# One pool of eight PSUM banks, and exponentials over any two of them, in an attention + Mish kernel

## The chip, the cores and the metric

The kernel runs on one core of a Trainium2 chip. The engines are TensorE (PE), VectorE (DVE), ScalarE (ACT), GpSimd (POOL) and SyncE (SP, which only issues DMAs here). PE writes its results to PSUM, which has eight banks of 512 float32 columns on each of 128 partitions; ACT and DVE read PSUM, POOL works on SBUF only. Each engine has its own instruction stream, which it works off in order, and the streams are tied together by semaphores. The metric is the device time of one execution in microseconds: 779.48 us, the median of three runs (779.46 to 780.76). The profiled execution took 773.49 us, with a span of 771.7 us from its first to its last instruction.

## The reference

With x of 2048 x 640, 32 heads of 20 columns, and a Mish feed-forward of width 1536:

```python
qkv = (x @ wqkv)                        # 640 -> 3 * 640, 32 heads of 20
scores = einsum("bhqd,bhkd->bhqk", q, k) * 20 ** -0.5
a = (softmax(scores) @ v) @ wo
h = x @ w1 + b1                         # 640 -> 1536
b = (h * tanh(softplus(h))) @ w2        # Mish, 1536 -> 640
g = sigmoid((x * gate_w).sum(-1))
out = g * a + (1 - g) * b
```

Softmax takes an exponential of 32 x 2048 x 2048 scores. That is the bulk of the element work, and it is what the change touches.

## The kernel before

**Tiling of the attention.** Heads are taken four at a time (p, eight quads), queries in chunks of 512 (c, four of them); a pair (p, c) is a group, 32 in all. For each of 16 key tiles (kt) the four heads of a group give four score tiles of 128 keys x 512 queries, each one PSUM bank. The scores of the four heads run on PE as four 32-row tiles of the array. Two heads' tiles make a unit: a slot of two neighbouring banks, 128 x 1024 float32. There are 1024 units.

**Two ways to an exponential.** A unit goes either to ACT, which takes the exponential of both banks in one instruction of 1024 columns (`poll_act`, L835, into a slot of `EA`), or to DVE, which writes a bit pattern that is a piecewise-linear exponential (`psum_chord`, L853, into `EC`); POOL then adds a constant twice to make two shifted copies (`gp_chord`, L864), and the three pieces are summed by PE like three key tiles. The latter are called chords below. 736 units go to ACT and 288 to DVE.

**PV.** PE multiplies the exponentials by V (`emit_pv`), four heads side by side as four 32-column tiles, and adds into one bank; a column of ones in `VA` yields the softmax denominators. DVE copies the bank out at the end of a group (L876).

**Banks before.** The eight banks have fixed uses: slots 0, 1 and 2 are banks 0-1, 2-3 and 4-5; bank 6 (`ACCB`) sums PV; bank 7 (`MISC`) takes all other matmuls (projections, w1, w2, wo, transposes), called pieces. In the opening banks 4 and 5 are lent to the pieces. All eight are parts of one tile, `K.ps`, and `EA` (8 slots) and `EC` (9) are two tiles.

**What sets the order.** `make_plan` plays the whole kernel through on a clock of assumed durations: `poll_pe`, `poll_act`, `poll_dve`, `poll_gp` and `poll_sp` each pick what their engine starts next, and `emit` records it. The recorded order is the order of the instructions in every stream. Waits are not written by hand: the framework compares the regions that instructions read and write, in program order, and puts semaphores where it finds a conflict. For PSUM it works by bank, and keeps apart two engines' accesses to one bank, two reads as well.

**Opening.** x comes in by five SP DMAs; PE transposes it (L240) and DVE copies it to `xT` (L245). The weights come through ACT's DMA queue (L1129 to L1139). `K_pad0` (L199) on DVE spreads the first quad's weights to 32-column strips before PE can make the first keys and queries. POOL fills `VA` with ones and clears `kT` and `qT`.

Of the kernel before, what the change touches and what calls it, by code (L numbers as in the profile page):

```python
# [10 lines left out]
P = 128  # L11
# [16 lines left out]
MISC, ACCB = 7, 6  # L28
NEA, NCH = 8, 9
# [22 lines left out]
for _c in range(NQC):  # L52
    GROUPS += [(6, _c), (7, _c)]
NG = len(GROUPS)
NU = NG * 32
# [3 lines left out]
    "thr": 326.27,  # L59
    "lead": 216.34,  # L60
    "dvw": 64.38,
    "gpmax": 2746.83,
    "gptwo": 3121.26,
    "urgent": 24.71,
    "kq": 3.96,
# [3 lines left out]
    "h0": 3.84,  # L69
    "h1": 14.84,  # L70
    "w0": 9.5,
    "w1": 21.29,
    "hl": 6.15,
    "wl": 5.27,
# [4 lines left out]
XAT = [3300.0, 4300.0, 6300.0, 8400.0, 10500.0]  # L79
# [66 lines left out]
def uinfo(n):  # L146
    g, k = divmod(n, 32)
    p, c = GROUPS[g]
    return g, p, c, k // 2, k % 2


def make_plan(K, par):
# [4 lines left out]
    stat = dict(act=0, dve=0, gp2=0, s4=0, s2=0, pv4=0, pv2=0, fill=0)  # L157
# [33 lines left out]
    pl.at(5500.0, lambda: dve_q.append(("fn", 950.0, K_pad0, lambda: pl.give("w0"))))  # L191
    pl.at(9000.0, lambda: pl.give("wv0"))
    pl.at(14000.0, lambda: pl.give("wk", "wq"))
    pl.at(18000.0, lambda: pl.give("wv"))
    pl.free["SP"] = 4000.0

    def K_pad0():
        for raw, dst in ((K.wk0, K.wkp), (K.wq0, K.wqp)):
            K.nc.vector.tensor_copy(  # L199
                out=dst.rearrange("p k (r d) -> p k r d", r=4)[:, :, :, 0:DH],  # L200
                in_=raw.rearrange("p k (r d) -> p k r d", r=4),
            )
# [118 lines left out]
    def add_v(j, t0, due):  # L321
# [18 lines left out]
        for i in range(nt):  # L340
            for kt in range(KT):
                pieces.append((max(w / 2.4, 50.0) + 2.0, "C", (lambda b, i=i, kt=kt: pc(i, kt, b)), ()))
# [48 lines left out]
    def add_wo(t, half, due):  # L391
        c, c0 = t // 4, half * 320

        def pc(j, b):
            n = 96 if j == 3 else P
            l = K.onc[0:n, c % 2, j, (t % 4) * P : (t % 4 + 1) * P]
            mm4(bank(b)[:, 0:320], l, K.wop[0:n, j, c0 : c0 + 320], j == 0, j == 5)
# [84 lines left out]
    ring_free = [0, 1]  # L482
    lent = [4, 5]
    misc_free = [MISC] + lent
    opn = {"lent": True, "tail": False, "back": 0}
    filled, flying = [], []
    land = [0.0]
    pair_free = {}
    eafree = list(range(NEA))
    ecfree = list(range(NCH))  # L490
    nxt, pv_g = [0], [0]
    acc_free = [True]
    pv_pend = {g: ([], []) for g in range(NG)}
    pv_left = {g: [16, 16] for g in range(NG)}
    nchord = {g: [0, 0] for g in range(NG)}
    first_w = {}
    mode = [None]
    recent = []
    tailq = []

# [6 lines left out]
    def unit_ready(n):  # L507
        g, p, c, kt, pair = uinfo(n)
        return ("k", p, kt // 4) in pl.tok and ("q", p, c) in pl.tok

    def emit_score(n, slot):
        g, p, c, kt, pair = uinfo(n)

        def fn():
            for t in range(2):
                r = 2 * pair + t
                mm(
                    K.ps[:, 2 * slot + t, :],
                    K.kT[32 * r : 32 * r + 32, p % 3, kt * P : (kt + 1) * P],
                    K.qT[32 * r : 32 * r + 32, p % 3, c * QC : (c + 1) * QC],  # L520
                    True,
                    True,
                    (32 * r, 0),
                )

        emit(fn)

    def scored(ns):
        for n, s in ns:
            flying.remove(n)  # L530
            filled.append((n, s))
            if n % 32 == 31:
                pl.give(("sdone", n // 32))

    def hurry():

        if filled or flying:
            return False
        ta = pl.free["ACT"]
        t2 = min(list(pair_free.values()) or [0.0])  # L540
        sw = 0.0 if mode[0] == "R" else 105.0
        if max(t2, pl.t) + 440.0 + sw <= ta + par["thr"]:
            return False
        return pl.t + 440.0 + sw + par["lead"] >= ta

    def try_score(idle=False):
        n = nxt[0]
        if n >= NU or not ring_free or not unit_ready(n):
            if n < NU and ring_free and n not in blk:
                blk[n] = [pl.t, pl.t]  # L550
            return False
        if n in blk:
            blk[n][1] = pl.t
        if len(ring_free) < 2 and not idle and not hurry():
            return False
        k = 1
        if n + 1 < NU and len(ring_free) >= 2 and unit_ready(n + 1):
            k = 2
        ns = [(n + i, ring_free.pop(0)) for i in range(k)]
        for u, s in ns:  # L560
            emit_score(u, s)
            flying.append(u)
        land[0] = pl.t + 440.0 + (105.0 if mode[0] != "R" else 0.0) if k == 2 else 0.0
        nxt[0] = n + k
        stat["s4" if k == 2 else "s2"] += 1
        pe_run("R", 217.0, lambda: scored(ns))
        return True

    def pv_usable(e):
        g, p, c, kt, pair = uinfo(e[0])  # L570
        return ("v", 0 if p == 0 else (1 if p < 4 else 2), kt) in pl.tok

    def emit_pv(g, items):
        if g not in first_w:
            first_w[g] = set()
            acc_free[0] = False
        todo = []
        for t in range(2):
            for pair, e in items:
                n, ap, rel, last = e  # L580
                _, p, c, kt, _ = uinfo(n)
                r = 2 * pair + t
                fin = last and pv_left[g][pair] == 1 and not pv_pend[g][pair]
                todo.append((r, kt, 4 * p + r, ap, t, r not in first_w[g], fin))
                first_w[g].add(r)

        def fn():
            for r, kt, h, ap, t, first, fin in todo:
                mm(
                    K.ps[32 * r : 32 * r + 32, ACCB, :],  # L590
                    K.VA[:, kt, h * VS : h * VS + 32],
                    ap()[:, t * QC : (t + 1) * QC],
                    first,
                    fin,
                    (0, 32 * r),
                )
# [3 lines left out]
        def done():  # L600
            for pair, e in items:
                e[2]()
                if e[3]:
                    pv_left[g][pair] -= 1
            if pv_left[g] == [0, 0] and pv_g[0] == g:
                pv_g[0] = g + 1
                gtimes.append(pl.t)
                dve_q.append(("acc", g))

        stat["pv4" if len(items) == 2 else "pv2"] += 1  # L610
        pe_run("C", 217.0, done)

    def try_pv(single=False):
        g = pv_g[0]
        if g >= NG or (g not in first_w and not acc_free[0]):
            return False
        items = [(pair, pv_pend[g][pair][0]) for pair in range(2) if pv_pend[g][pair] and pv_usable(pv_pend[g][pair][0])]
        if not items:
            return False
        if len(items) < 2 and not single and pv_left[g][1 - items[0][0]] > 0:  # L620
            return False
        for pair, e in items:
            pv_pend[g][pair].pop(0)
        emit_pv(g, items)
        return True

    def try_misc(lim):
# [3 lines left out]
        if not misc_free or lim is None:  # L631
            return False
        for k, m in enumerate(misc[:40]):
            if m.due > nxt[0] + lim:
                break
            if pl.has(m.need):
                if hasattr(m, "key"):
                    if not stg_free:
                        continue
                    stg_of[m.key] = stg_free.pop(0)  # L640
                misc.pop(k)
                m.bank = misc_free.pop(0)
                started.append(m)
                return run_piece(m)
        return False

    def run_piece(m):
# [11 lines left out]
        pe_run(md, dur, done)  # L659
        return True  # L660

    def lent_back():
        opn["back"] += 1
        if opn["back"] == 2:
            ring_free.append(2)

    def misc_done(m):
        b = m.bank
        if b in lent and not opn["lent"] and not opn["tail"]:
            lent_back()  # L670
        else:
            misc_free.append(b)
        pl.give(*m.gives)
        if m.name == "xt15":
            opn["lent"] = False
            for x in [x for x in misc_free if x in lent]:
                misc_free.remove(x)
                lent_back()
        if m.name.startswith("w2."):
            for q in range(2):  # L680
                if ("w2done", q) not in pl.tok and all(("w2e", t, hh) in pl.tok for t in range(8 * q, 8 * q + 8) for hh in range(2)):
                    pl.give(("w2done", q))
                    if q == 1:
                        load_wo()
# [497 lines left out]
```

## Time and profile before

| | us |
|---|---|
| median of three runs | 779.48 |
| profiled execution / its span | 773.49 / 771.7 |
| ACT busy | 719.0 (93%) |
| PE busy (matmuls are pipelined, ends modelled) | 736.6 (95%) |
| POOL busy | 665.6 (86%) |
| DVE busy | 499.1 (65%) |
| ACT: 736 exponentials, mean 1041 ns each, together | 689.1 |
| DVE: 288 chords, mean 1223 ns each | 351.8 |
| POOL: 576 shifted copies, mean 1047 ns each | 602.9 |

The mean of one instruction is from its start to its end; successive exponentials overlap a little, so 736 of them take 689.1 us, or 0.936 us each. A busy share says how long an engine had something in flight. For PE it is larger than the time in which PE streams columns, since a matmul's end is modelled and four small tiles run side by side. What an engine waited for is read from the idle time before its instructions.

### The profile page before, as it was taken

Reading aid. Unit: us, or ns where it says so; the run is one execution under the profiler, and the core shown is the slowest. Engines: PE = TensorE matmul, PEld = TensorE weight load, DVE = VectorE, ACT = ScalarE, POOL = GpSimd, SP = SyncE. Lnnn points to the kernel's source line nnn. Section 1 sums busy time; section 2 is a strip of 40 time slices with the busy share of each in tenths; the row PEclk is TensorE's granted clock in tenths of the full one; section 3 lists DMA queues with packets and bytes.
Section 4 is the critical chain, followed back from the end, with each engine's and each line's share of the span. In section 5 each row is a group of like instructions: output and inputs, shape, how many; then the busy total and the mean of one; then the engine's idle time right before and its main releaser. Section 6 shows DMA issues by size and latency. Waiting matters only on the chain.

```text
span 771.7 us, 24991 instructions
## 1 busy us (share of the span) xinstructions
PE 736.6 (95%) x10492; PEld 261.3 (34%) x10492; DVE 499.1 (65%) x588; ACT 719.0 (93%) x757; POOL 665.6 (86%) x627
## 2 busy tenths in 40 slices
PE   4899999999999999999999999999999999999996
PEld 2333332332233433333233323224333333333234
DVE  5676566666667666676656667667666655666573
ACT  1599999999999999999999999999999999999992
POOL 9378777889888999899999878988999999999994
PEclk9999999999999999999999999999999999999999
DMA  9231211110111010111211111012201003122112
GB/s 294 95 119 59 79 41 31 41 38 21 34 27 41 23 29 20 44 40 34 80 29 29 33 50 38 17 27 74 82 28 48 25 28 89 50 76 68 58 52 79
DMA packets 45682, 41.86 MB, mean 54 GB/s; under 512 B 20080, under 2 KB 39200, under 8 KB 45568
## 3 DMA queue, kind: packets, MB, share of 16 engines
q1 hardware_dynamic: 40976, 37.59, 16.5%
q10 hardware_dynamic: 4592, 2.66, 1.2%
q8 instruction: 82, 1.34, 0.7%
q14 instruction: 32, 0.26, 0.1%
HBM read 27.59 MB, written 12.38 MB: 52 GB/s over the span
## 4 chain that ended last, share of the span: by engine, by line
PE 59%; POOL 20%; ACT 7%; DVE 5%; issue 5%; DMA 3%; SPq 0%; DVEq 0%; POOLq 0%; ACTq 0%
PE ps L230 59%; POOL EC L864 19%; ACT EA L835 7%; DVE EC L853 3%; DMA b1bf<-in_B_b_dram 2%; POOL ons L1014 1%; DVE accs L876 1%; DMA act<-in_A_x_dram 1%; POOL R L1014 0%; PE ps L240 0%; DVE act L353 0%; DVE stg L285 0%; DMA den<-accs 0%; SPq L993 0%; DVE ost L400 0%
## 5 line engine op out<-in xcount | busy, mean ns | idle before, releaser
L835 ACT ACTIVATE EA<-ps 128x1024 bf16<-128x1024 f32 x736 | 689.1, 1041 | 35.9 <-PE ps L230 31.9
L864 POOL TENSOR_SCALAR EC<-EC 128x1024 uint16<-128x1024 uint16 x576 | 602.9, 1047 | 92.8 <-DVE EC L853 46.7
L853 DVE TENSOR_SCALAR EC<-ps 128x1024 uint16<-128x1024 f32 x288 | 351.8, 1223 | 203.3 <-PE ps L230 129.2
L230 PE MATMUL ps<-qT,kT 32*128 32x512 bf16 x2048 | 289.1, 384 | 7.7 <-ACT EA L835 4.1
L230 PE MATMUL ps<-EC,VA 128*32 128x512 bf16 x1728 | 237.7, 384 | 6.2 <-POOL EC L864 4.6
L230 PE MATMUL ps<-EA,VA 128*32 128x512 bf16 x1472 | 210.2, 384 | 0.4 <-DVE accs L876 0.2
L230 PEld LDWEIGHTS <-kT 32*128 32x128 bf16 x2048 | 77.2, 91 | 253.6 <-issue 250.3
L230 PEld LDWEIGHTS <-VA 128*32 128x32 bf16 x3200 | 82.6, 94 | 113.8 <-issue 98.9
L230 PE MATMUL ps<-R,act 128*32 128x320 bf16 x1536 | 83.0, 302 | 0.3 <-DVE bst L372 0.3
L230 PE MATMUL ps<-xT,R 128*32 128x512 bf16 x960 | 77.1, 383 | 0.6 <-DVE act L353 0.3
L230 PEld LDWEIGHTS <-R 128*32 128x32 bf16 (+1 forms) x1728 | 41.2, 95 | 45.5 <-issue 33.1
L230 PEld LDWEIGHTS <-act 128*32 128x32 bf16 x1536 | 37.0, 95 | 32.0 <-issue 24.2
L353 DVE TENSOR_SCALAR act<-ps,b1f 128x512 bf16<-128x512 f32 x48 | 35.8, 746 | 8.5 <-PE ps L230 8.4
L230 PE MATMUL ps<-R,R 128*32 128x320 bf16 (+1 forms) x768 | 40.0, 302 | 0.5 <-DVE R L974 0.5
L230 PE MATMUL ps<-wv,xT 128*32 128x81 bf16 (+2 forms) x960 | 34.2, 257 | 0.9 <-DVE kT L262 0.5
L285 DVE CAST stg<-ps 128x512 bf16<-128x512 f32 (+1 forms) x40 | 27.3, 683 | 10.9 <-PE ps L230 10.5
L230 PE MATMUL ps<-xT,wk 128*32 128x512 bf16 (+1 forms) x360 | 32.5, 383 | 0.8 <-DVE bst L372 0.3
L1014 POOL TENSOR_TENSOR ons<-accs,rb 128x512 bf16<-128x512 f32 x24 | 30.6, 1275 | 2.0
L230 PE MATMUL ps<-xT,wq 128*32 128x512 bf16 x400 | 31.2, 383 | 0.4 <-DVE VA L332 0.4
L876 DVE COPY accs<-ps 128x512 f32<-128x512 f32 x32 | 21.9, 685 | 7.9 <-PE ps L230 7.5
L230 PEld LDWEIGHTS <-xT 128*32 128x32 bf16 x960 | 18.5, 96 | 13.6 <-issue 11.7
L372 DVE TENSOR_SCALAR bst<-ps,og 128x320 bf16<-128x320 f32 x32 | 17.4, 544 | 8.7 <-PE ps L230 8.0
(62 smaller groups left out, 179.1 us busy)
## 6 DMA issues: line engine op xcount, KB each, us to landing
rb<-rd_d SPq DMA_DIRECT2D x124, 64.0 KB
qd<-stg SPq DMA_DIRECT2D x20, 128.0 KB
b_d<-bst SPq DMA_DIRECT2D x16, 160.0 KB
bst<-b_d SPq DMA_DIRECT2D x16, 160.0 KB
out_dram<-ost SPq DMA_DIRECT2D x16, 160.0 KB
kT<-kd SPq DMA_DIRECT2D x28, 80.0 KB
qT<-qd SPq DMA_DIRECT2D x28, 80.0 KB
kd<-stg SPq DMA_DIRECT2D x16, 128.0 KB
```

The source lines that it names most:

```text
L230: K.nc.tensor.matmul(o, lhsT=l, rhs=r, start=first, stop=last, tile_position=pos, skip_group_check=True)
L285: K.nc.vector.tensor_copy(out=K.stg[0:w, s, :], in_=bank(b)[0:w, :])
L353: K.nc.vector.tensor_scalar(out=K.act[:, f, (c % 2) * QC : (c % 2 + 1) * QC], in0=bank(b), scalar1=K.b1f[:, f : f + 1], scalar2=None, op0= ...
L372: K.nc.vector.tensor_scalar(out=K.bst[:, t % 3, c0 : c0 + 320], in0=bank(b)[:, 0:320], scalar1=K.og[:, t : t + 1], scalar2=None, op0=ALU.mult,
L835: lambda: K.nc.scalar.activation(K.EA[:, e, :], K.ps[:, 2 * slot : 2 * slot + 2, :].rearrange("p b n -> p (b n)"), ACT.Exp, scale=SCALE)
L853: lambda: K.nc.vector.tensor_scalar(out=K.EC[:, e, :], in0=K.ps[:, 2 * slot : 2 * slot + 2, :].rearrange("p b n -> p (b n)"), scalar1=CH_M ...
L864: K.nc.gpsimd.tensor_scalar(out=K.EC[:, e, :], in0=K.EC[:, e0, :], scalar1=float(CH_ADD[k]), scalar2=1.0, op0=ALU.add, op1=ALU.mult)
L876: emit(lambda: K.nc.vector.tensor_copy(out=K.accs[:, g % 2, :], in_=K.ps[:, ACCB, :]))
L1014: gp_q.append((1350.0, lambda: K.nc.gpsimd.tensor_tensor(out=dst(), in0=K.accs[:, b, :], in1=K.rb[:, b, :], op=ALU.mult), lambda: pl.give( ...
```

## The change

It does five things.

1. Scores are handled by the bank. A unit is now one head's tile in one bank (2048 units). All eight banks are one list, `pool`: scores, pieces and the PV sum take banks from it as they come free, up to four scores a visit of PE.
2. An ACT exponential takes any two filled banks with one instruction, by a stride between them: `K.ps[:, b0 : b1 + 1 : b1 - b0, :]`. Its output goes to any two slots likewise.
3. A chord is one bank on DVE (128 x 512); two of them share one POOL instruction per shifted copy, over two slots with a stride.
4. `EA` and `EC` become one tile `E` of 35 slots of 512 columns.
5. Opening: the spreading of the first weights goes from DVE to ACT, ahead of ACT's later DMA issues; POOL sets only the `VA` columns that V does not overwrite; the clearing of rows 96 to 127 of `onc` and of the same rows of `wop` is new on POOL, and wo's pieces use all 128 rows.

The parameters of the plan change with it. Cut to its core:

```diff
-MISC, ACCB = 7, 6
-NEA, NCH = 8, 9
+NE = 35
-NU = NG * 32
+NU = NG * 64
...
-    pl.at(5500.0, lambda: dve_q.append(("fn", 950.0, K_pad0, lambda: pl.give("w0"))))
+    pl.at(5800.0, lambda: pl.give("w0"))
...
-    ring_free = [0, 1]
-    lent = [4, 5]
-    misc_free = [MISC] + lent
+    pool = list(range(8))
...
-    def emit_score(n, slot):
+    def emit_score(n, b):
...
+            mm(
+                bank(b),
...
     def try_score(idle=False):
...
+        k = len(pool)
+        g = pv_g[0]
+        if g not in accb:
+            k -= 1
+        if not started and next_misc(par["resv"]) is not None:
+            k -= 1
+        k = min(k, 4)
...
+        while len(ns) < k and n + len(ns) < NU and unit_ready(n + len(ns)):
+            ns.append((n + len(ns), pool.pop(0)))
...
     def poll_act():
-            emit(
-                lambda: K.nc.scalar.activation(
-                    K.EA[:, e, :], K.ps[:, 2 * slot : 2 * slot + 2, :].rearrange("p b n -> p (b n)"), ACT.Exp, scale=SCALE
-                )
-            )
...
+            us = sorted((filled.pop(0) for _ in range(min(2, len(filled)))), key=lambda x: x[1])
+            es = sorted(efree.pop(0) for _ in us)
+            k, b0, b1, e0, e1 = len(us), us[0][1], us[-1][1], es[0], es[-1]
+
+            def fn():
+                src = K.ps[:, b0 : b1 + 1 : max(b1 - b0, 1), :]
+                dst = K.E[:, e0 : e1 + 1 : max(e1 - e0, 1), :]
+                K.nc.scalar.activation(dst, src, ACT.Exp, scale=SCALE)
...
-                in0=K.ps[:, 2 * slot : 2 * slot + 2, :].rearrange("p b n -> p (b n)"),
+                K.nc.vector.tensor_scalar(
+                    out=K.E.bitcast(U16)[:, es[k][i], :],
+                    in0=K.ps[:, b, :],
...
     def gp_chord(src, dst, k):
         K.nc.gpsimd.tensor_scalar(
+            out=slots(dst), in0=slots(src), scalar1=float(CH_ADD[k]), scalar2=1.0, op0=ALU.add, op1=ALU.mult
...
-    tl("EA", [P, NEA, 2 * QC], BF16)
-    tl("EC", [P, NCH, 2 * QC], U16)
+    tl("E", [P, NE, QC], BF16)
...
     nc.scalar.activation(K.dmy, K.dmy, ACT.Exp)
+    for raw, dst in ((wk0, K.wkp), (wq0, K.wqp)):
+        nc.scalar.activation(
+            dst.rearrange("p k (r d) -> p k r d", r=4)[:, :, :, 0:DH],
+            raw.rearrange("p k (r d) -> p k r d", r=4),
+            ACT.Copy,
+        )
     nc.scalar.dma_start(K.wv[:, :, 0:V0], cols(2 * D, 2 * D + V0))
...
-    nc.gpsimd.memset(K.VA[:, 0:4, :], 1.0)
-    nc.gpsimd.memset(K.VA[:, 4:16, :], 1.0)
+    nc.gpsimd.memset(K.VA[:, :, 0 : H * VS].rearrange("p t (h d) -> p t h d", d=VS)[:, :, :, DH:VS], 1.0)
+    for h in (4, 16, H):
+        nc.gpsimd.memset(K.VA[:, :, h * VS : h * VS + 12], 1.0)
```

How the instructions count, before and after, in the built programs:

| engine, work | before | after |
|---|---|---|
| ACT exponentials | 736 of 1024 columns | 732 of two banks, 3 of one |
| of these over neighbouring banks | 736 | 144 |
| DVE chords | 288 of 1024 | 647 of 512 (66 banks get two) |
| POOL shifted copies | 576 of 1024 | 547 of two slots, 2 of one |
| PE scores, matmuls / visits | 2048 / 710 | 2048 / 729 |
| PE PV matmuls | 3200 | 3210 |
| PE matmuls by zero (fills) | 72 | 36 |

## The prediction

> **What bounds the kernel now.** I read the busy shares first, then the groups of instructions, then ACT's own timeline.
>
> ```profile
> PE 736.6 (95%) x10492; PEld 261.3 (34%) x10492; DVE 499.1 (65%) x588; ACT 719.0 (93%) x757; POOL 665.6 (86%) x627
> ...
> L835 ACT ACTIVATE EA<-ps 128x1024 bf16<-128x1024 f32 x736 | 689.1, 1041 | 35.9 <-PE ps L230 31.9
> ...
> L876 DVE COPY accs<-ps 128x512 f32<-128x512 f32 x32 | 21.9, 685 | 7.9 <-PE ps L230 7.5
> ```
>
> PE's 95% is modelled overlap: 20 matmuls of 512 columns at 29.07 below take 1.25 us, four abreast, so a row of four streams for (1.25 - 0.39) / 4 = 0.215 us. All matmuls of the kernel before at that rate (by width) stream for 536 us. ACT is the bound: 689.1 / 736 = 0.936 us per exponential, idle only 35.9 us ahead of them, of which these rows of its timeline show the large part:
>
> ```profile
> 17.50 1.94 ACT L835 ACTIVATE EA<-ps 128x1024 bf16<-128x1024 f32 x2 [14.20 <-PE ps L230]
> 22.10 5.60 ACT L835 ACTIVATE EA<-ps 128x1024 bf16<-128x1024 f32 x6 [2.67 <-PE ps L230]
> 34.15 17.12 ACT L835 ACTIVATE EA<-ps 128x1024 bf16<-128x1024 f32 x18 [6.44 <-PE ps L230]
> ...
> 407.29 88.34 ACT L835 ACTIVATE EA<-ps 128x1024 bf16<-128x1024 f32 x94 [0.29 <-PE ps L230]
> ```
>
> From 34 to 755 us ACT is 98% busy. It runs 94 exponentials without a stop because PE, DVE and ACT work on different slots at the same time. So what can be won is the opening and some 12 us of small gaps; what can be lost is that overlap.
>
> **The change part by part.**
>
> *Counts.* ACT: 732 exponentials of two banks and 3 of one for 736, 732 x 0.936 + 3 x 0.5 = 686.7, -2.4 us. The strided form has no row; the nearest are Mish over 12 runs of 256 columns (four in 10.72 us at 245.82, 0.87 ns per column and row) and the exponential itself (0.936 us per 1024, 0.91 ns). The runs cost Mish nothing to be seen; I take 0, ends -10 and +35 us (0.05 us on 669). DVE: 647 chords at the 0.685 us of the 512-column copy above are 443 us for 351.8, +91; DVE then works 586 of 771 us, hidden behind ACT's 98%; were ACT faster it would be next. POOL: 548 copies for 576 at 1.047 us, -29 us, hidden; its new small memsets (1.49 us for the 1536 columns at L1144) are covered by that. PE: 2.5 more PV rows, 9 fewer fills, 19 more score visits at 0.1 us: under 2 us. All hidden as long as ACT's stream runs on.
>
> *Opening.*
>
> ```profile
> 7.10 4.92 DVE L199 COPY wkp<-wk 128x400 bf16<-128x400 bf16 x1
> ...
> 12.07 2.33 PE L230 MATMUL ps<-xT,wkp 128*32 128x512 bf16 x20 [3.18 <-DVE wkp L199]
> ...
> 17.40 0.45 PE L240 MATMUL ps<-ident,act 128*128 128x128 bf16 x5
> 20.54 0.44 PE L240 MATMUL ps<-ident,act 128*128 128x128 bf16 x5 [2.69 <-DVE xT L245]
> ...
> 29.07 1.25 PE L230 MATMUL ps<-xT,wkp 128*32 128x512 bf16 x20
> ```
>
> The first keys wait for the DVE copy until 12.02. On ACT two copies of 400 columns cost about 0.5 us each (ACT's 320-column `otmp` takes 0.53) once the weights have landed, between 4 and 7.1 us; PE could begin at 7.2, when the first four tiles of `xT` are done: -4.9 us. Of the gaps of 2.67 and 6.44 us, which wait for later keys, between none and all may go: I take -3, so -8 in all, ends 0 and -14. ACT's five weight DMAs (L1135 to L1139) now stand behind the copies, 4 to 6 us later; the first use of `wq` and `wv` was at 28 and 31 us, so this hides. POOL's shorter memsets end earlier, but its first chord came only at 31 us: 0.
>
> *The waits that strided exponentials bring.* This is the large term. The framework makes a wait from regions. I read, in the order of the built program, which instruction each wait names. An exponential over banks b0 and b1 is guarded as if it touched every bank between them. 588 of the 735 exponentials have banks in between. One place shows it: exponential 362 reads banks 1 and 7 and waits for the last PV matmul put into bank 5 before it; the next PE instruction in order, a w2 matmul into bank 4, waits for exponential 362 to end, and so does DVE's next chord, of bank 6; exponential 363 (banks 0 and 3) waits for scores that stand behind that w2 matmul, and for a chord of bank 2 that stands behind the chord of bank 6. PE and DVE work in order, so everything behind the waiting instruction waits too.
>
> To count it, I followed from each exponential all waits back through the other engines (with what stands ahead in their order) to the newest exponential that must have ended. Before: that is the one just ahead for 3 of 736, two back for 606, three for 125. After: just ahead for 517 of 735, two back for 207. With the same order but each bank guarded for itself, it would be 3 and 674. So in 517 places ACT must end, another engine must do its piece, and only then ACT goes on. The prices:
>
> ```profile
> 35.07 3.77 ACT L835 ACTIVATE EA<-ps 128x1024 bf16<-128x1024 f32 x4
> ...
> 36.14 0.39 PE L230 MATMUL ps<-qT,kT 32*128 32x512 bf16 x2 [0.15 <-ACT EA L835]
> ```
> ```profile
> 545.91 0.39 PE L230 MATMUL ps<-qT,kT 32*128 32x512 bf16 x2
> ...
> 546.40 1.02 ACT L835 ACTIVATE EA<-ps 128x1024 bf16<-128x1024 f32 x1 [0.38 <-PE ps L230]
> ```
> ```profile
> 759.49 0.40 PE L230 MATMUL ps<-EC,VA 128*32 128x512 bf16 x4
> ...
> 759.94 0.69 DVE L876 COPY accs<-ps 128x512 f32<-128x512 f32 x1 [3.63 <-PE ps L230]
> ```
>
> The first exponential of the row at 35.07 lasts 1.02 us, to 36.09, and the score that waits for it starts at 36.14: from ACT's end to PE's start 0.05 us. From PE's start to the reader's start it is 0.45 us (0.49 and 0.45 here). An exponential lasts 1.03 us from start to end.
>
> - 371 places by PE alone. Their stretches of PE, from the first instruction that waits for the old exponential to the one that the new one waits for, hold 2,482 matmuls, 157.5 us of streaming, 0.425 each. Pitch: 1.03 + 0.05 + (0.425 - 0.215) + 0.45 + 0.07 for a change between score and other tiles (a score visit of 0.39 is followed after 0.32, not 0.215) = 1.81 instead of 0.936: 0.87 x 371 = 323 us.
> - 79 by PE and then DVE: 1.03 + 0.05 + 0.55 + 1.1 chords x 0.69 + 0.05 = 2.43, 1.49 x 79 = 118 us.
> - 40 by one DVE read: 1.85, 0.91 x 40 = 36 us.
> - 27 by two or three DVE reads: about 1.64 x 16 + 2.7 x 11 = 56 us.
>
> Together +533 us. Lower end: shortest exponential (1.006), no passing time, 0.43 from PE to ACT, no change of tiles: 1.64 and 2.13, 1.70, 2.4, loss 261 + 94 + 31 + 40 = +426. It can't be less while the waits are in the program. Upper end: the stretches may in turn wait for DVE, POOL or slots (POOL's copies now often wait for PE to free a slot: 411 waits on PE for 25), and the 207 places two back may lose something: I allow 0.25 us on all 735, +180.
>
> The Trainium skill, "PSUM — Partial Sum Buffer", on bank collisions, says to guard PSUM by bank and quadrant, and that accesses to different banks run clean. By that rule the banks in between need no guard; guarded so, the order would have 3 such places, and the sum would be the third rival's.
>
> Sum: 771.7 - 2.4 - 8 + 533 + 2 = 1296 us of span. The profiled time stands 1.8 us above its span and the median 6 us above that: 1304. Rounded 1300. Ends: 771.7 - 13 - 14 + 426 + 8 = 1179; two thirds of the upper allowance, 120 us, make 1420.
>
> **The rivals.**
>
> 1. *The same alternation, and PE falls to its slow rate as well.* Two rows of 20 equal matmuls above differ: 2.33 us after 3 us without a matmul, 1.25 later. PE streams 544 of 1300 us (42%). Against: after a gap of 2.69 us at 20.54 five transposes took 0.44, as before it, and the new gaps are about 1 us. Slow for half the time, the stretches (239 us of streaming in all classes, and 0.2 more on 470 ends) cost +165: 1465. The Trainium skill, "TensorE: Matmul & The Clock Gate", Part 1: The HAM clock gate, has the clock drop after an idle window of 3.4 us; by that gaps of 1 us keep it up, and the row at 20.54 agrees.
> 2. *Cheaper alternation.* Many of the waits named may be met by the time they are read, if PE and DVE lag less than the program allows. Against: in these 517 places the chain starts at the end of the exponential just ahead, so nothing can be early. Half price would be 1040.
> 3. *Faster.* The guards in between don't act at run time, and the opening decides: 779.5 - 8 - 2.4 - some 6 of the small gaps = 763. It decides when fewer than some 15 exponentials pay 0.87 us. For it: nothing in the rows; the waits of the kernel before are in its trace (596 waiting instructions on ACT, of 603 in its program).
> 4. *DVE the bound, no guards.* 586 us on DVE plus its waits for PE (129.2 before): about 790.
>
> **How the numbers follow.** Forecast 0.80, rival 1 0.07, rival 2 0.07, rival 3 0.05, rival 4 0.01. The range 1180 to 1420 is the forecast's own. Faster by over 0.2%: 0.05; within 0.2%, about what a measurement here can tell from no change: 0.01; slower: 0.94.
>
> **What would show it.** ACT idle some 500 us ahead of the exponentials, released by PE and DVE; PE idle ahead of matmuls "<-ACT", in the before 4.3 us, now hundreds; rows of one to three exponentials instead of 94; one exponential still 1.03 us; PE's rows of 20 at 1.25 us; the first exponential before 14 us. The prediction is wrong if ACT's rows are as long as before, or if the strided exponential itself lasts longer.

## The result, and the profile after

The changed kernel takes 1615.1 us, the median of four runs (1613.8 to 1621.9), beside 779.5 us for the kernel before on the same chip: 2.074 times as long, with a 95% interval of 2.067 to 2.080. The forecast was 1300 with a range to 1420. The direction was right, and the size was missed by 315 us. One of the ten executions of the first experiment's kernel below took 1038.5 us at a mean clock of 0.56, and its ratio leaves that one out.

The profiled execution has a span of 1612.0 us. Its page, first the busy shares and the granted clock of TensorE in 40 slices (5 is half speed), then the costliest groups with their idle time ahead:

```profile
PE 1180.3 (73%) x10466; PEld 305.0 (19%) x10466; DVE 579.5 (36%) x945; ACT 777.4 (48%) x758; POOL 629.6 (39%) x604
...
PEclk8755567576666755555565775575657555556767
...
L849 ACT ACTIVATE E<-ps 128x1024 bf16<-128x1024 f32 x735 | 746.2, 1022 | 815.1 <-PE ps L233 616.4
...
L988 DVE TENSOR_SCALAR E<-ps 128x512 uint16<-128x512 f32 x647 | 434.4, 688 | 829.9 <-PE ps L233 619.5
```

The idle time ahead of ACT's exponentials has grown from 35.9 to 815.1 us, which is 779 of the 840 us that the span has grown by. One exponential still lasts 1.02 us, as one by itself did before (the row at 546.40 in the prediction), so the strided form itself costs nothing. No engine is busy throughout: PE's 73% holds matmuls that last longer (a PV matmul 0.55 us on average for 0.38), since the mean clock of the execution is 0.623 (0.999 before). The waits (us in total, times, longest) name the partners:

```profile
ACT E L849 <- PE ps L233: 616.4, 529, 6.3
...
PE ps L233 <- ACT E L849: 416.7, 443, 2.2
...
DVE E L988 <- ACT E L849: 179.3, 87, 4.5
ACT E L849 <- DVE E L988: 156.8, 106, 2.8
```

ACT waits for PE and DVE, and PE and DVE wait for ACT. "PE waits for ACT" was 4.3 us in all before. In the timeline of 800 us (start, duration, operation, idle before it) one sees the turns. ACT's rows first, then PE's in the same stretch:

```profile
804.55 1.02 ACT L849 ACTIVATE E<-ps 128x1024 bf16<-128x1024 f32 x1 [1.53 <-PE ps L233]
807.43 1.02 ACT L849 ACTIVATE E<-ps 128x1024 bf16<-128x1024 f32 x1 [1.86 <-PE ps L233]
810.35 1.02 ACT L849 ACTIVATE E<-ps 128x1024 bf16<-128x1024 f32 x1 [1.90 <-PE ps L233]
```
```profile
805.62 0.62 PE L233 MATMUL ps<-E,VA 128*32 128x512 bf16 x4 [1.13 <-ACT E L849]
806.17 0.61 PE L233 MATMUL ps<-qT,kT 32*128 32x512 bf16 x3
806.71 0.62 PE L233 MATMUL ps<-xT,wk 128*32 128x512 bf16 x4
808.50 0.62 PE L233 MATMUL ps<-E,VA 128*32 128x512 bf16 x4 [1.18 <-ACT E L849]
```

The exponential at 804.55 ends at 805.57, PE starts at 805.62, works through three rows of tiles, and the next exponential starts at 807.43. That is the alternation that was forecast, with rows of one exponential where 94 ran without a stop before. A row of four matmuls starts 0.55 us before the next one, where about 0.32 was to be seen at full clock for such changes of tiles. After its first data has come PE is never idle for longer than 2.2 us, and yet its clock is at half for most of the time.

The opening did as forecast. ACT copies the first weights at 4.48 and 5.83 us, PE begins the first keys at 7.21 (7.2 was forecast, 12.07 before), and the first exponential starts at 12.68 (17.50 before). ACT's rows, and PE's one:

```profile
4.48 0.54 ACT L1238 ACTIVATE wkp<-wk 128x400 bf16<-128x400 bf16 x1 [1.18 <-DMA wk<-in_A_wqkv_dram]
...
12.68 1.02 ACT L849 ACTIVATE E<-ps 128x1024 bf16<-128x1024 f32 x1 [6.32 <-PE ps L233]
14.45 5.85 ACT L849 ACTIVATE E<-ps 128x1024 bf16<-128x1024 f32 x7 [0.75 <-DVE xT L248]
```
```profile
7.21 2.32 PE L233 MATMUL ps<-xT,wkp 128*32 128x512 bf16 x20 [0.58 <-DVE xT L248]
```

### The profile page after: what moved, and what is told of

Read it like the earlier page. It is cut to its first block, busy times and chain, and to the rows that moved or that the text cites. A ratio compares the mean times of both kernels' runs of the same rounds, so it can differ in the third digit from the quotient of the medians.

```text
span 1612.0 us, 25631 instructions
## 1 busy us (share of the span) xinstructions
PE 1180.3 (73%) x10466; PEld 305.0 (19%) x10466; DVE 579.5 (36%) x945; ACT 777.4 (48%) x758; POOL 629.6 (39%) x604
## 3 DMA queue, kind: packets, MB, share of 16 engines
q10 hardware_dynamic: 4592, 2.66, 0.6%
## 4 chain that ended last, share of the span: by engine, by line
PE 29%; ACT 14%; DVE 3%; issue 3%; POOL 1%; ACTq 0%; DMA 0%; DVEq 0%; SPq 0%; POOLq 0%
PE ps L233 29%; ACT E L849 14%; DVE E L988 3%; POOL E L875 1%; ACTq L849 0%; DVE act L356 0%; DMA bst<-b_d 0%; DVE stg L288 0%; DVE accs L931 0%; DVE ost L402 0%; POOL ost L795 0%; DVEq L988 0%; POOL R L1087 0%; DVEq L1287 0%; SPq L186 0%
## 5 line engine op out<-in xcount | busy, mean ns | idle before, releaser
L849 ACT ACTIVATE E<-ps 128x1024 bf16<-128x1024 f32 x735 | 746.2, 1022 | 815.1 <-PE ps L233 616.4
L875 POOL TENSOR_SCALAR E<-E 128x1024 uint16<-128x1024 uint16 x549 | 573.8, 1045 | 962.6 <-DVE E L988 510.3
L988 DVE TENSOR_SCALAR E<-ps 128x512 uint16<-128x512 f32 x647 | 434.4, 688 | 829.9 <-PE ps L233 619.5
L233 PE MATMUL ps<-E,VA 128*32 128x512 bf16 x3210 | 430.4, 550 | 185.4 <-ACT E L849 185.2
L233 PE MATMUL ps<-qT,kT 32*128 32x512 bf16 x2048 | 440.9, 536 | 122.3 <-ACT E L849 120.2
L233 PE MATMUL ps<-R,act 128*32 128x320 bf16 x1536 | 118.4, 401 | 38.4 <-ACT E L849 38.4
L233 PE MATMUL ps<-xT,R 128*32 128x512 bf16 x960 | 116.4, 528 | 26.4 <-ACT E L849 25.8
L233 PEld LDWEIGHTS <-R 128*32 128x32 bf16 x1728 | 42.9, 104 | 139.0 <-issue 133.1
L233 PE MATMUL ps<-R,R 128*32 128x320 bf16 x768 | 53.2, 380 | 13.2 <-ACT E L849 12.6
L233 PE MATMUL ps<-xT,wk 128*32 128x512 bf16 (+1 forms) x360 | 53.9, 569 | 10.6 <-ACT E L849 10.6
```

Source lines behind the costliest of these rows:

```text
L233: K.nc.tensor.matmul(o, lhsT=l, rhs=r, start=first, stop=last, tile_position=pos, skip_group_check=True)
L849: K.nc.scalar.activation(dst, src, ACT.Exp, scale=SCALE)
L875: K.nc.gpsimd.tensor_scalar(out=slots(dst), in0=slots(src), scalar1=float(CH_ADD[k]), scalar2=1.0, op0=ALU.add, op1=ALU.mult)
L988: K.nc.vector.tensor_scalar(out=K.E.bitcast(U16)[:, es[k][i], :], in0=K.ps[:, b, :], scalar1=CH_MUL, scalar2=CH_OFF + CH_ADD[k], op0=ALU.mult,
```

## The experiments

Two questions were open after the result. Is it the guard of the banks in between that makes the engines take turns, or the handling by the bank (more chords on DVE, one pool, visits of up to four scores)? And what are the 315 us that the forecast lacked: PE's clock, or turns that were not counted? Kernels of which one time is given ran once beside runs of the kernel before; the others were timed in several rounds.

**The same order with no exponential over distant banks.** Pairs of banks that are not neighbours (588 of 735) become two instructions of one bank each; the order of everything else stays.

```diff
+                if b1 - b0 > 1:
+                    K.nc.scalar.activation(K.E[:, e0, :], K.ps[:, b0, :], ACT.Exp, scale=SCALE)
+                    K.nc.scalar.activation(K.E[:, e1, :], K.ps[:, b1, :], ACT.Exp, scale=SCALE)
+                    return
```

> The changed kernel in its own order, but an exponential over two banks that are not neighbours is issued as two instructions of one bank each (588 become 1176; 144 stay whole). No instruction spans a bank that it does not read, so the waits on banks in between are gone: in the built program no exponential but 3 needs the one just ahead of it to have ended by way of another engine (517 of 735 in the changed kernel). Theory A (the waits on banks in between make ACT, PE and DVE take turns, and the PE clock falls because PE then idles): ACT is the bound again, 144 x 0.94 + 1179 x some 0.5 + 27 for Mish = 750 us of work, span 765 to 830 us, granted clock above 0.95, ACT idle under 70 us. Theory B (handling by the bank is itself the cost: 647 DVE instructions for 288, one pool, POOL waiting for slots): at least 1200 us, since all of that is still there.

Measured: 775.67 us, 0.9965 of the kernel before [0.9941, 0.9990]. The places where an exponential needs the one just ahead fall from 517 to 3 in the built program. Its page, busy shares and ACT's groups:

```profile
PE 758.4 (98%) x10466; PEld 240.9 (31%) x10466; DVE 562.0 (73%) x945; ACT 742.2 (96%) x1346; POOL 629.8 (81%) x604
...
L848 ACT ACTIVATE E<-ps 128x512 bf16<-128x512 f32 x588 | 498.0, 849 | 6.8 <-PE ps L233 6.6
L849 ACT ACTIVATE E<-ps 128x512 bf16<-128x512 f32 x588 | 503.3, 858 | 0.0
...
L853 ACT ACTIVATE E<-ps 128x1024 bf16<-128x1024 f32 (+1 forms) x147 | 174.7, 1236 | 6.9 <-PE ps L233 6.9
```

ACT's idle time is back at 14 us. All else of the change is in this kernel: the pool, the chords by the bank, the visits of PE, the opening. So the kernel that handles scores by the bank is level with the kernel before, and the whole loss of 840 us hangs on the span of the strided reads. It holds the gain of the opening, though, which alone gives 767.5 us (below): the handling by the bank and the split pairs together cost some 8 us. The mean of 849 ns is lengthened by overlap; successive single exponentials start some 0.48 us apart in the timeline.

**The kernel before with spread slots.** The order is untouched; a slot is banks s and s+3 instead of 2s and 2s+1. Every exponential and every chord then has two banks in between, which belong to the two other slots.

```diff
-                    K.ps[:, 2 * slot + t, :],
+                    K.ps[:, slot + 3 * t, :],
...
-                    K.EA[:, e, :], K.ps[:, 2 * slot : 2 * slot + 2, :].rearrange("p b n -> p (b n)"), ACT.Exp, scale=SCALE
+                    K.EA[:, e, :].rearrange("p (b n) -> p b n", b=2), K.ps[:, slot : slot + 4 : 3, :], ACT.Exp, scale=SCALE
...
```

> The kernel before in its own order, with one thing changed: a slot's two banks are s and s + 3 instead of 2s and 2s + 1, so exponentials and chords read them with a stride and span the two banks in between. Units, sizes and counts are those of before. In the built program 693 of 736 exponentials need the one just ahead to have ended by way of PE or DVE (3 before). Theory A: alternation, and the PE clock falls with it: 1500 to 1750 us, granted clock 0.5 to 0.75. Theory C (alternation alone, the clock has no part): about 1470 us (491 x 0.70 + 99 x 1.91 + 56 x 1.4 + 46 x 1.9 on 772), clock above 0.95. Theory B: 770 to 800 us, as nothing is handled by the bank here.

Measured: 1734.39 us, span 1732.5, clock 0.593. The program has 693 places of 736 where the exponential just ahead must have ended, for 3 before. Its waits:

```profile
ACT EA L835 <- PE ps L230: 595.3, 546, 2.5
...
ACT EA L835 <- DVE EC L853: 311.4, 147, 10.8
```

ACT waited 546 + 147 = 693 times, as often as the program has such places. A numbering of banks alone, with not one instruction more and the plan as it was, makes the kernel 2.2 times as long. With the first experiment this shows the cause from both sides.

**PE's clock by itself.** A kernel that computes nothing of the reference (its output is zeros): PE does g rows of four matmuls of 512 columns, ACT then reads both banks with one exponential, PE goes on when that has ended. Stages of some 60 us with g = 16, 12, 8, 6, 4, 3, 2, 1 and back up.

```diff
+    for g in STAGES:
+        for _ in range(cycles(g)):
+            groups(g)
+            exps()
```

> A small kernel that computes none of the reference (its output is zeros): PE and ACT take turns strictly, g rows of four matmuls of 512 columns and then one exponential of two banks that waits for them, which the next matmuls wait for. g goes 16, 12, 8, 6, 4, 3, 2, 1 and back up to 16, some 60 us each. At the full clock a turn should last about 1.03 + 0.05 + 0.45 + 0.215 (g - 1) us, so PE streams 68, 62, 52, 45, 35, 29, 21, 12% of the time and is idle 1.1 to 1.5 us in each turn. If the clock goes by the share of streaming: full at g of 12 and more, half at g of 4 and less, the edge in between, perhaps lower on the way down than on the way up. If only a long idle stretch (more than 3 us) lowers it: full in all stages.

Measured, the median from one exponential to the next, in us:

| rows | 16 | 12 | 8 | 6 | 4 | 3 | 2 | 1 |
|---|---|---|---|---|---|---|---|---|
| going down | 4.82 | 3.96 | 3.09 | 2.66 | 3.08 | 2.65 | 2.23 | 1.80 |
| going up | 4.82 | 3.96 | 3.09 | 2.66 | 3.08 | 2.65 | 2.23 | 1.80 |

At 6 rows and above a turn is 1.37 + 0.2157 g, below it 1.37 + 0.427 g. The forecast's price of a turn without its 0.07 for a change of tiles, of which there is none here, is 1.03 + 0.05 + 0.45 + 0.215 (g - 1) = 1.315 + 0.215 g. It is 0.06 us short, as long as the clock is up. Where it falls, PE's rows in the timeline show, around the step from six rows to four:

```profile
250.49 1.48 PE L50 MATMUL ps<-xs,w 128*32 128x512 bf16 x24 [1.18 <-ACT e L61]
253.15 1.48 PE L50 MATMUL ps<-xs,w 128*32 128x512 bf16 x24 [1.18 <-ACT e L61]
255.81 1.05 PE L50 MATMUL ps<-xs,w 128*32 128x512 bf16 x16 [1.18 <-ACT e L61]
258.04 1.90 PE L50 MATMUL ps<-xs,w 128*32 128x512 bf16 x16 [1.18 <-ACT e L61]
261.12 1.90 PE L50 MATMUL ps<-xs,w 128*32 128x512 bf16 x16 [1.18 <-ACT e L61]
```

The gap ahead of each row is 1.18 us on both sides of the step, and the same 16 matmuls take 1.05 and then 1.90 us. What has changed is the length of PE's rows, and with it the share of the time in which PE streams columns: 6 x 0.2157 / 2.66 = 49% holds the clock, 4 x 0.2157 / 2.23 = 39% loses it, within the first such turn. On the way up it stays at half with four rows (4 x 0.427 / 3.08 = 55% at the slow rate) and comes back with six (2.56 / (1.37 + 2.56) = 65%). The windows of that kernel around the two steps (span of the window, then PE, PEld, DVE, ACT and POOL busy, then the granted clock):

```profile
240.00:260.00 20.00, 11.66 (x176) 5.12 (x169) 0.00 (x0) 7.16 (x7) 0.00 (x0) 0.94 0.01 2
260.00:280.00 20.00, 11.79 (x101) 3.98 (x104) 0.00 (x0) 7.16 (x7) 0.00 (x0) 0.50 0.00 0
...
740.00:760.00 20.00, 11.96 (x104) 4.15 (x107) 0.00 (x0) 7.04 (x7) 0.00 (x0) 0.50 0.00 1
760.00:780.00 20.00, 11.73 (x184) 5.21 (x176) 0.00 (x0) 7.16 (x7) 0.00 (x0) 0.93 0.00 1
```

In this kernel the share and the length of the rows change together. The traces of the large kernels tell them apart. In each of them the granted clock is full or half and nothing else, and every change lies a whole number of stretches of 3.413 us after the first one. Seven such stretches of the changed kernel, with the same columns:

```profile
812.19:815.60 3.41, 3.41 (x27) 0.65 (x25) 1.38 (x2) 1.92 (x2) 1.18 (x2) 0.50 0.00 0
815.60:819.02 3.42, 3.08 (x46) 1.06 (x44) 1.69 (x3) 2.51 (x4) 1.96 (x2) 1.00 0.13 46
819.02:822.43 3.41, 1.91 (x26) 0.66 (x26) 1.83 (x4) 2.41 (x3) 2.09 (x2) 1.00 0.00 0
822.43:825.84 3.41, 2.22 (x22) 0.63 (x18) 1.03 (x2) 1.56 (x3) 1.85 (x2) 0.50 0.02 2
825.84:829.26 3.42, 3.42 (x30) 0.64 (x23) 1.38 (x3) 1.72 (x2) 1.33 (x3) 0.50 0.01 3
829.26:832.67 3.41, 1.16 (x15) 0.31 (x11) 1.15 (x2) 1.59 (x2) 1.00 (x1) 1.00 0.13 48
832.67:836.08 3.41, 1.71 (x11) 0.34 (x11) 0.69 (x1) 1.34 (x2) 0.00 (x0) 0.50 0.00 0
```

PE's busy time here has modelled ends; by the widths of the matmuls it streams 85 and 83% of the two stretches ahead of a rise, 41 and 19% of the two ahead of a drop, and 71% of the one that holds the clock. The eight traces with a changing clock (the changed kernel, the spread one with its four fills, the far pairs strided, and this small one) have 2,298 stretches at full clock, 285 of them ahead of a drop. One limit on the share, at some 45%, puts 108 of them on the wrong side; the best limit on the longest row of matmuls puts 213 there, and the best on the longest gap 237. At half clock a rise goes with a share above some 83% in the same way (84 of 1,289 on the wrong side). So it is the share of a stretch that goes with the clock, and the two limits lie far apart.

The forecast itself had PE streaming 42% of its 1300 us. That lies below the limit of 45%.

**The clock given back, in the spread kernel.** Rows of four zero matmuls, which add nothing to the bank of the PV sum (no exponential spans it), keep PE busy: four or two rows ahead of nearly every score visit, and later two or four behind it.

```diff
+        gf = pv_g[0]
+        if gf < NG and len(first_w.get(gf, ())) == 4 and pv_left[gf] != [0, 0]:
+            for _ in range(EXTRA):
+                emit(zeros)
         for u, s in ns:
             emit_score(u, s)
```

> The same as the spread kernel, with four more rows of four matmuls by zero ahead of nearly every score visit (712 x 4 rows, 618 us of PE streaming at the full clock; they add nothing to the PV sum), most of it at a time when PE would idle beside an exponential. Theory A (the clock falls because PE streams too small a share of the time, and costs time on the path): the granted clock rises above 0.9 and the span is shorter than that of the spread kernel although PE does more than twice the work, 1400 to 1550 us. Theory C: the span is no shorter than that of the spread kernel, and the clock does not move.

> The spread kernel again (before, slots of banks s and s + 3), with two rows of matmuls by zero ahead of a score visit instead of four. With four the clock rose from 0.593 to 0.98 but the span only fell from 1732 to 1722 us. If four rows (0.86 us of PE a visit) were late for the score they stand ahead of and so gave back what the clock won: with two (0.43 us) the clock stays above 0.9 and the span falls to 1480 to 1620 us. If the clock has no part in the span: about 1720 again.

> The spread kernel of before's order (1734 us, mean clock 0.593), with two rows of four zero matmuls BEHIND each score visit in place of ahead of it (which gave 1655 at clock 0.917). They add zero to the bank of the PV sum, which no exponential spans, and PE does them while ACT works on the scores just made. Theory A (the slow clock is the missing part: a row costs 0.427 us in place of 0.216 on the path of each turn): the clock stays mostly up, little of the rows lies on the path, and the time falls to 1350 to 1500. Theory B (the turns are passing times, and the clock counts for little; the missing part is turns that were not counted): it stays above 1600 although the clock is up.

> As before it with four rows behind each score visit (0.86 us at the full rate, a little less than one exponential of 1.02 us). Theory A: the clock is at 0.97 or more and the time is at or below that of two rows where these left the clock lower, 1350 to 1500; where PE has more to do behind an exponential than the rows leave room for, up to 100 us more. Theory B: above 1600.

| rows a visit | none | 2 ahead | 2 behind | 4 ahead | 4 behind |
|---|---|---|---|---|---|
| time, us | 1734.4 | 1655.2 | 1657.6 | 1723.6 | 1732.2 |
| mean clock | 0.593 | 0.917 | 0.925 | 0.980 | 0.983 |
| ACT waits for PE, times | 546 | 544 | 547 | 549 | 549 |

All four gave less than a gain by the clock alone had promised; of the last two, the letter of the expectation goes to the rival, above 1600. But the rows are not free where they stand. Two rows are 5,656 matmuls more, 305 us of streaming at the full rate, and from two rows to four the time rises by 68 (ahead) and 75 us (behind) with the clock nearly up in both. So PE with two rows does 305 us more, and the kernel is 79 us faster. Carried on in a straight line to no rows, full clock would be at about 1655 - 70 = 1585 us, so the clock would account for some 150 of the 1734. This is an estimate: it takes the first two rows to cost what the next two did, and the clock with two rows is not quite up. At least 79 us is the clock; how much more was not measured.

In the turns of the kernel with two rows ahead, now at full clock, the forecast's other price can be read:

```profile
701.38 1.02 ACT L844 ACTIVATE EA<-ps 128x1024 bf16<-128x1024 f32 x1 [0.55 <-PE ps L231]
702.94 1.02 ACT L844 ACTIVATE EA<-ps 128x1024 bf16<-128x1024 f32 x1 [0.54 <-PE ps L231]
705.80 1.02 ACT L844 ACTIVATE EA<-ps 128x1024 bf16<-128x1024 f32 x1 [1.84 <-DVE EC L862]
707.28 1.02 ACT L844 ACTIVATE EA<-ps 128x1024 bf16<-128x1024 f32 x1 [0.46 <-PE ps L231]
710.23 1.02 ACT L844 ACTIVATE EA<-ps 128x1024 bf16<-128x1024 f32 x1 [1.93 <-DVE EC L862]
```

A turn by PE alone is 1.48 to 1.56 us in these rows (1.90 on average over the trace at full clock), one by PE and then DVE's chord of two banks 2.86 to 2.95 (2.89 on average); the forecast's way of counting gives 1.03 + 0.05 + 0.55 + 1.24 + 0.05 = 2.92 for the latter.

**Neighbours where they can be had, else two instructions; and the same order with far pairs strided.** The plan looks up to four filled banks ahead for a neighbour and knows the measured costs (0.936 us for a pair, 0.49 for one bank). The second kernel has the first one's order and makes the 384 far pairs strided again, so that the two differ by the guards and by ACT's counts. There, 294 exponentials need the one just ahead, and 392 the one two back.

```diff
+            us = [filled.pop(0)]
+            if filled:
+                j = [j for j in range(min(len(filled), int(par["look"]))) if abs(filled[j][1] - us[0][1]) == 1]
+                us.append(filled.pop(j[0] if j else 0))
...
-                if far:
+                if False:
```

> A kernel meant to beat both: the changed kernel, where an exponential takes a neighbouring bank if one is filled (319 of one instruction over two neighbours) and else two instructions of one bank each; the plan's assumed durations are set to measured ones (ACT 0.936 and 0.49 us, DVE 0.645, POOL 1.06) and its parameters chosen anew. No exponential but 2 needs the one just ahead of it by way of another engine. ACT's work is 319 x 0.936 + 781 x 0.49 + 27 = 708 us for 742 in the run with two instructions throughout; DVE takes 612 banks and more. If ACT is the bound: 745 to 762 us. If DVE or PE takes over: 765 to 780.

> The same kernel and order as the one before in this list, but a pair that is not neighbouring is again one instruction with a stride, as in the changed kernel. In the built program 294 exponentials need the one just ahead by way of PE or DVE (517 in the changed kernel, 2 without strides). If each such place costs what the prediction reckoned at the full clock, 533 / 517 = 1.03 us: 755 + 303 = about 1060 us, and PE streams 545 / 1060 = 51%, which in the small turn-taking kernel was enough to keep the full clock once it was up. If each costs what the changed kernel paid, (1612 - 775) / 517 = 1.62 us: 1230 us with a low clock.

Measured: 771.0 us for the first, 0.9903 [0.9871, 0.9934] of before, less than hoped for; 1290.38 us for the second, clock 0.756, above both figures expected. So 294 places cost 519 us, 1.77 each, where the forecast's prices give about 1.0. Its waits:

```profile
ACT E L862 <- PE ps L234: 397.0, 394, 3.9
...
ACT E L862 <- DVE E L1001: 101.2, 84, 2.9
```

ACT waited 478 times, 184 more than there are places with the exponential just ahead. In the changed kernel it waited 529 + 106 = 635 times for 517 such places, 118 more; in the spread kernel 693 times for 693. So the surplus is found where many exponentials need the one two back (392, 207 and 22), which in the kernel before (606 of them) cost nothing.

**The opening alone.** The kernel before with ACT's copies of the first weights and POOL's smaller memsets, nothing else.

```diff
+    for raw, dst in ((wk0, K.wkp), (wq0, K.wqp)):
+        nc.scalar.activation(
+            dst.rearrange("p k (r d) -> p k r d", r=4)[:, :, :, 0:DH],
+            raw.rearrange("p k (r d) -> p k r d", r=4),
+            ACT.Copy,
+        )
```

> The kernel before in its own order with the opening's changed operations alone: the first weights are spread by two ACT copies instead of two DVE copies, and POOL sets only the VA columns that V does not overwrite. The prediction's -4.9 us for this part: first exponential near 12.6 us instead of 17.5, time 770 to 775 us, as the gaps of 2.7 and 6.4 us behind it wait for later keys and stay. If ACT's weight DMAs, now behind the copies, come too late: no gain, 778 us or more.

Measured: 767.52 us, 0.9864 [0.9841, 0.9886] of before, better than expected and the fastest kernel of this study. ACT's long rows at the start:

```profile
14.33 7.44 ACT L831 ACTIVATE EA<-ps 128x1024 bf16<-128x1024 f32 x8 [7.86 <-PE ps L226]
28.13 17.12 ACT L831 ACTIVATE EA<-ps 128x1024 bf16<-128x1024 f32 x18 [6.36 <-PE ps L226]
```

The first exponential is 3.2 us earlier (4.9 was expected), the gap of 2.67 us is gone, the one of 6.4 stays: the row of 18 starts 6.0 us earlier than before, and the profiled spans differ by 5.7 us (766.0 for 771.7). The medians differ by 10.8, because the profiled execution of before was one of its faster ones; where the other 5 us lie isn't shown.

## Why the prediction was right, and where it failed

*The mechanism: right.* Guards on the banks in between, 517 places, ACT taking turns with PE and DVE. Taking the spans away with the order kept gives 775.7; putting them into the kernel before gives 1734. Rival 3 (the guards don't act) and rival 4 (DVE the bound: 562 us busy and 171 idle ahead of its chords in the first experiment, with no loss) fall.

*The places: right in kind, too few.* 517 were counted, ACT waited 635 times for exponentials' banks. The 207 places two back stood in the forecast with an allowance only, outside the sum.

*The price of a turn at full clock: right to some 0.1 us.* 1.37 + 0.2157 g measured for 1.315 + 0.215 g, and 2.89 us for a turn through DVE's chord of two banks for 2.92 by the same sum. In the changed kernel itself, from the start of one exponential to that of the next, the 93 turns that PE ended while the clock was full took 1.70 us on average, for 1.81; the 35 that DVE ended took 2.01, for 2.37 as the mean of the forecast's three classes with DVE. At these two means all its 654 turns (528 by PE, 126 by DVE) would lose 539 us, for the 533 of the sum. That more turns, each cheaper, come to the same is luck. Rival 2 (half the price) falls.

*The step that failed: "Against: after a gap of 2.69 us at 20.54 five transposes took 0.44, as before it, and the new gaps are about 1 us", and with it the 0.07 for rival 1.* The forecast took the clock to depend on the length of one gap. So the sum held nothing for a slow clock. The gaps are indeed short, at most 2.2 us, and the clock was at half for (1 - 0.623) x 2 = 75% of the time. The Trainium skill's rule in "TensorE: Matmul & The Clock Gate", Part 1: The HAM clock gate, of an idle window of 3.4 us, was taken as support; the runs here show the clock lost at gaps of 1.18 us when PE streams 39% of the time, and in the changed kernel after stretches of 3.413 us that stream 13 to 51%. Here the measurement decides. One row after one gap could not tell a rule of gaps from a rule of shares; the forecast's own 42% was the number to worry about. Rival 1 had the mechanism, with half of the time at the slow rate and 1465.

*What the terms measure.* Rival 1's own working gives +165 for half of the time, so for 75% of it 165 x 0.754 / 0.5 = 249, and 1296 + 249 = 1545 of the span's 1612. That leaves 67 us for the 118 further waits, 0.57 each. The same prices for the other two kernels:

| | forecast's prices, full clock | clock term | sum | measured span | left |
|---|---|---|---|---|---|
| changed kernel | 1296 | 249 | 1545 | 1612.0 | 67 |
| spread slots | 1498 | 231 | 1729 | 1732.5 | 4 |
| far pairs strided | 1070 | 96 | 1166 | 1288.6 | 123 |

(For the spread slots: 771.7 + 491 x 0.73 + 145 x 1.98 + 51 x 1.44 + 5 x 1.44, the stretches being 0.276 us; the clock 0.814 x (0.98 x 160 + 0.2 x 636). For the far pairs: 769.5 + 223 x 0.90 + 41 x 1.49 + 19 x 0.91 + 21 for places with two or more DVE reads; the clock 0.488 x (0.98 x 147 + 0.2 x 264).) What is left is nothing in the kernel with 22 places two back, and 67 and 123 us in those with 207 and 392: 0.32 and 0.31 us a place. So it fits that at half clock a turn over two exponentials no longer passes in two exponentials' time. That this is the cause was only argued from three sums; and the clock term of the spread kernel, 231, lies above the 150 that the rows of zeros suggest and the 79 that they show. There the split between clock and further waits is open by some 100 us.

For the changed kernel its own turns narrow it: those at half clock took 2.32 us by PE (378 turns) and 2.63 by DVE (73), 0.62 more than at full clock in both, with as much of PE's work in them (0.61 and 0.67 us of streaming at the full rate, for 0.61 and 0.66). At 0.62 us for these 451 turns the clock would account for some 280 us. This is an estimate, since the turns at full and at half clock are not the same ones; with the 249 above it says that the clock is most of the 315 us that the forecast lacked.

Zero rows in the changed kernel itself were not tried: all its eight banks lie in some span, so that the rows would wait in turn. A strided exponential that is guarded only by its own two banks was not tried either.

*The small terms.* ACT's counts and the strided form: 1.022 us for 1.041, no cost. DVE's chords 434.4 us for 443 forecast, hidden. The opening: first exponential at 12.68, "before 14" as said, worth 6 us alone by the spans and 10.8 by the medians, for 8. Of the marks set down beforehand, those on ACT's waits, PE's waits, rows of one, and 1.03 us an exponential held; "PE's rows of 20 at 1.25 us" was the one on the clock, and rows of four tell that it was slow.

*What would have been faster.* With the guards out of the way the two by-bank kernels, which hold the opening too, reach 775.7 and 771.0; the opening without the pool of banks reaches 767.5 (beside 771.0 on the same chip). So the pool brings nothing here, and what the change had to give was its opening.

## What to carry to other kernels

Before an access is made to stride over buffers that others use, read in the built program which instruction each wait names: a guard by span turns independent buffers into one, and the count of places where an engine must wait for its own last instruction's readers says how bad it is. When a change makes engines take turns, work out the share of time in which PE will stream, not only the length of its gaps: if it falls below some 45%, price the rows at both rates. And test the parts of a change apart; here one of them was a gain, hidden under a loss some hundred times its size.

## What the runs showed of the hardware

- In these traces TensorE's granted clock is full or half, changes only on a grid of 3.413 us, and goes by the share of such a stretch in which PE streams, with a memory: best parted at some 45% for the drop and some 83% for the rise. Neither limit is sharp: in the changed kernel the stretches ahead of a drop stream 13 to 51%, those that keep the full clock 35 to 100%. In the kernel of strict turns the clock held at 49% of a turn, fell at 39%, stayed down at 55% at the slow rate and came back at 65%, where the stretch ahead of the rise streams 75%. The gap was 1.18 us throughout, and the kernel before kept the full clock over a gap of 2.69 us, so no single gap decides it.
- Four tiles of 512 columns side by side take 0.2157 us at full and 0.427 at half clock.
- More work can make a kernel faster: 5,656 added matmuls (305 us of streaming at the full rate) took 79 us off the spread kernel.
- An exponential over two banks with a stride takes as long as one over two neighbours: by itself 1.02 us in both. Two exponentials of one bank take 0.96 us one after the other, for 0.936 of one over two banks: splitting a pair costs ACT only some 3%.
